# A list scheduler in place of a hand-written order, in the attention stage of an attention and routed-experts kernel

## The chip, the cores and the metric

The kernel runs on one core of one Trainium2 chip. The time is the device time of one execution in microseconds (us). The kernel before takes 1050.81 us (median of 4 runs, 1050.44 to 1051.66).

Engines: PE is TensorE's matmuls, PEld its weight loads, DVE is VectorE, ACT is ScalarE, POOL is GpSimd, SP is the engine that issues most loads. In this kernel TensorE writes its results to a memory called PSUM, in banks, and other engines copy them from there to SBUF. A name such as L247 is a line of the kernel whose profile is shown; the two kernels number their lines differently.

## The reference, cut to what matters

```python
# attention: batch 8, heads 8, 512 local and 32 global tokens, head size 64
out_g = softmax(scale * q_g @ [k_g, k_l].T) @ [v_g, v_l]          # global rows see everything
s_ll  = where(abs(i - j) <= 32, scale * q_l @ k_l.T, -1e9)         # local rows: a band of 65
out_l = softmax([scale * q_l @ k_g.T, s_ll]) @ [v_g, v_l]          #   and the 32 global keys
x = concat(out_g, out_l).reshape(4352, 512)                        # tokens x model
# routing: exp(x @ w_gate), 8 iterations of row and column normalising, P is 4352 x 8
# experts: out = sum_e P[:, e] * (relu(x @ w1[e]) @ w2[e]),  w1 512x1024, w2 1024x512
```

## The kernel before

Attention is worked off in 32 head pairs (two heads side by side); four pairs make a block, which is one batch entry. For each pair TensorE transposes q and k into one PSUM tile `pt`; ACT copies the q half and DVE the k half to SBUF; TensorE makes scores; ACT takes exponentials; DVE multiplies the band mask in; TensorE multiplies by v (`attend`); DVE normalises; TensorE transposes back to `xT`, the input of the experts.

Expert 0 needs no routing weights before its end, so its 560 big matmuls serve as filler for TensorE while attention waits for ACT and DVE. After attention come the rest of the filler, with the balancing (the 8 normalisations) hidden under it, and then experts 1 to 7, "the expert stage".

```python
def transposes(p):
    pt = ps_t.tile([P, 2, Sl], FP16, tag="t", name="pt")          # one buffer, one PSUM bank
    for so in range(4):
        nc.tensor.transpose(pt[:, 0, P * so : P * (so + 1)], nat[b, "q"][...], identity)
    for so in range(4):
        nc.tensor.transpose(pt[:, 1, P * so : P * (so + 1)], nat[b, "k"][...], identity)
    t = qkT[p] = wk.tile([P, 2, Sl], FP16, tag="qkT", bufs=3, name="qkT")
    for j, copy in enumerate((nc.scalar.copy, nc.vector.tensor_copy)):   # q by ACT, k by DVE
        copy(out=t[:, j, :]..., in_=pt[:, j, :]...)
# ... cut ...
def attend(p):                                                     # 28 small matmuls
    for i in (0, 1):
        for m in range(NM):        # 8 of 128x128 against 65 columns
            nc.tensor.matmul(po[:, i, VC * m : VC * (m + 1)], um(i, m, P * m - lo[m], P), vts[b % 2][:, j + m, :], ...)
    for m in range(NM - 1):        # 12 of 32 columns, the rims of the band
        ...
    for m in range(NM):            # 8 for the global keys
        ...
# ... cut ...
        READY = HP + 2
        DRAIN = (HP, 2 * HP)       # before blocks 1 and 2 the pipeline of pairs is emptied
        for s in range(NP + 3):
            have = b - 1 if s < 3 * HP else (s - READY) // HP      # which blocks' filler may run
            FA = 3.45 if s < 3 * HP else 2.3
            def fill_in():
                filler(FA / 4, have)                               # filler units by a credit of us
            # ... scores, fill_in, gate, transposes, fill_in, back, scores, masks, fill_in, attend ...
```

The softmax here doesn't subtract the row's maximum and nothing guards it: scores larger than these inputs give would overflow.

## Time and profile before

| stretch of the kernel before | us | what it is |
|---|---|---|
| 0 to 38.5 | 38.5 | first four pairs, no filler yet |
| 38.5 to 70.1 | 31.6 | blocks 1 and 2 start, two drains |
| 70.1 to 212.8 | 142.7 | the steady part of attention, with filler |
| 212.8 to 263.6 | 50.8 | rest of the filler, balancing hidden |
| 263.6 to 1048.8 | 785.2 | expert stage |

First the profile page of the kernel before, parts 1 and 2: busy time with its share of the span and the number of instructions, then the span in 40 equal slices, a digit being the busy share in tenths (PEclk: the granted TensorE clock in tenths).

```profile
PE 1015.0 (97%) x10063; PEld 831.2 (79%) x10063; DVE 652.3 (62%) x1366; ACT 458.5 (44%) x840; POOL 45.8 (4%) x80
...
PE   5888999999999999999999999999999999999997
...
PEclk9989999999999999999999999999999999999999
```

Next the busy time by stretch, kernel before. After the stretch and its length, each engine has its busy us with the number of instructions; PEclk is the granted clock, 1.00 being full; then come DMA share and GB/s.

```profile
core 0: us, PE busy (x) PEld busy (x) DVE busy (x) ACT busy (x) POOL busy (x), PEclk, DMA share, GB/s
0.00:38.50 38.50, 22.56 (x306) 14.17 (x306) 20.13 (x40) 16.95 (x35) 7.11 (x24) 1.00 1.06 244
38.50:70.10 31.60, 26.61 (x350) 14.75 (x349) 17.28 (x33) 17.92 (x40) 0.41 (x1) 0.84 0.67 208
70.10:212.80 142.70, 136.95 (x2022) 79.07 (x2021) 103.06 (x199) 93.07 (x208) 20.42 (x31) 1.00 0.58 155
212.80:263.60 50.80, 49.47 (x257) 24.79 (x254) 29.56 (x62) 23.97 (x46) 6.76 (x10) 1.00 0.85 180
263.60:1048.80 785.20, 779.45 (x7140) 698.38 (x7138) 482.32 (x1033) 306.62 (x511) 11.15 (x15) 1.00 0.27 74
```

The expert stage is three quarters of the time and is not touched. The clock column hides a cold phase: clock records begin at 42.8 us, and before that matmuls start at about double the distance (107 ns against 56 from one transpose of q or k to the next).

Over the whole steady part TensorE's pieces make 111.1 of the 142.7 us of the chain, DVE's 18.4 and ACT's 9.6.

The last view of the kernel before is the timeline of PE around one attend (start us, us, engine line operation). Note the starts of the lines L287 and L290.

```profile
95.01 0.42 PE L281 MATMUL po<-vt,u 128*128 128x65 f16 x8
95.36 0.20 PE L287 MATMUL po<-vt,u 128*32 128x65 f16 x1
95.36 0.20 PE L290 MATMUL po<-vt,u 128*32 128x65 f16 x1
95.40 0.20 PE L287 MATMUL po<-vt,u 128*32 128x65 f16 x1
95.40 0.20 PE L290 MATMUL po<-vt,u 128*32 128x65 f16 x1
...
95.65 0.29 PE L296 MATMUL po<-vga,ugk 32*128 32x65 f16 x8
95.88 0.31 PE L312 MATMUL gbank<-vt,u 128*32 128x65 f16 x16
```

The small matmuls start in pairs at nearly the same time and then nothing starts for about 0.03 us. The 28 matmuls from 95.01 to 95.88 us take 0.87 us, 31 ns each on average; but over the trace the median distance to the next start is 33 ns for L281, 4 ns for L287, 33 ns for L290 and 15 ns for L296, which sums to 0.61 us. Most of the rest lies where one kind of matmul follows another: by the trace 0.12 us pass from the last start of L281 (95.24) to the first of L287 (95.36), and as much again before L296 and before L312. A median over a line doesn't see these three pauses.

### The profile page before, as it was taken

How to read it: one execution, taken by the hardware profiler on the slowest of the kernel's cores; microseconds unless marked ns; L12 is line 12 of the kernel's file. 1: busy time of each engine (PE TensorE's matmuls, PEld its weight loads, DVE VectorE, ACT ScalarE, POOL GpSimd, SP SyncE). 2: the span in 40 equal slices, each digit the busy share in tenths (PEclk: the TensorE clock that was granted, in tenths of full speed). 3: DMA queues.
4: the chain of work that ended last, by engine and by line, in shares of the span. 5: the costliest groups of instructions: out<-in, count | busy, mean ns of one | idle time of the engine just before them, and what ended most of it. 6: DMA issues, size and time to landing. Idle time of an engine off the chain costs nothing.

```text
span 1048.8 us, 23363 instructions
## 1 busy us (share of the span) xinstructions
PE 1015.0 (97%) x10063; PEld 831.2 (79%) x10063; DVE 652.3 (62%) x1366; ACT 458.5 (44%) x840; POOL 45.8 (4%) x80
## 2 busy tenths in 40 slices
PE   5888999999999999999999999999999999999997
PEld 3445555544888888888888888888888888888886
DVE  5557788564455575555555555567766666666665
ACT  4456776644544444444444444433333333333332
POOL 2002020020100000000000000020000000000000
PEclk9989999999999999999999999999999999999999
DMA  9949792195821122122211121294321321321321
GB/s 260 243 127 219 232 249 73 42 195 145 159 61 62 61 61 62 61 61 61 61 62 62 62 61 61 62 179 93 92 76 56 96 72 56 95 72 56 95 73 41
DMA packets 111175, 105.33 MB, mean 100 GB/s; under 512 B 16720, under 2 KB 86368, under 8 KB 111072
## 3 DMA queue, kind: packets, MB, share of 16 engines
q1 hardware_dynamic: 85168, 77.75, 24.4%
q0 software_dynamic: 22016, 21.51, 11.7%
q10 hardware_dynamic: 3888, 4.59, 1.3%
q8 instruction: 78, 1.28, 0.5%
q14 instruction: 25, 0.20, 0.1%
HBM read 93.73 MB, written 26.88 MB: 115 GB/s over the span
## 4 chain that ended last, share of the span: by engine, by line
PE 91%; DVE 5%; ACT 2%; issue 1%; DMA 0%; DVEq 0%; SPq 0%; ACTq 0%
PE ph L601 40%; PE acc L626 34%; PE ph L109 5%; PE py L121 5%; PE sc L247 1%; DVE u L259 1%; DVE xn L303 1%; PE pt L232 1%; PE sc L251 1%; ACT u L255 1%; PE gbank L329 1%; PE pt L230 1%; PE po L281 1%; PE po L287 1%; PE po L296 0%
## 5 line engine op out<-in xcount | busy, mean ns | idle before, releaser
L603 ACT ACTIVATE h<-ph 128x512 f16<-128x512 f32 x476 | 284.1, 597 | 464.5 <-PE ph L601 432.5
L601 PE MATMUL ph<-xp,w1e 128*128 128x256 f16 x3808 | 435.0, 273 | 0.0
L601 PEld LDWEIGHTS <-w1e 128*128 128x128 f16 x3808 | 372.6, 98 | 43.3
L611 DVE TENSOR_TENSOR s<-h 128x512 f16<-128x512 f16 x595 | 210.1, 420 | 269.3 <-ACT h L603 269.3
L626 PE MATMUL acc<-wb,s 128*128 128x256 f16 x2380 | 279.3, 273 | 0.0
L626 PEld LDWEIGHTS <-s 128*128 128x128 f16 x2380 | 232.9, 98 | 26.9
L589 DVE TENSOR_TENSOR xp<-xT,pb 128x1024 f16<-128x1024 f16 x119 | 145.0, 1219 | 35.7 <-DMA pb<-ptd 35.7
L651 DVE TENSOR_TENSOR o<-o,acc 128x256 f32<-128x256 f32 (+1 forms) x306 | 134.5, 504 | 5.1 <-PE acc L626 1.5
L626 PE MATMUL acc<-wb,h 128*128 128x256 f16 x952 | 123.4, 273 | 0.0
L626 PEld LDWEIGHTS <-h 128*128 128x128 f16 x952 | 93.2, 98 | 10.8
L109 PE MATMUL ph<-xT,w 128*128 128x512 f16 (+1 forms) x288 | 73.1, 380 | 2.3 <-DVE hT L92 1.4
L121 PE MATMUL py<-w,hT 128*128 128x512 f16 x272 | 69.7, 381 | 0.9 <-ACT ys L96 0.9
L255 ACT ACTIVATE u<-sc 128x480 f16<-128x480 f32 (+1 forms) x128 | 59.5, 520 | 16.8 <-PE sc L251 16.1
L109 PEld LDWEIGHTS <-w 128*128 128x128 f16 x288 | 26.2, 101 | 27.5 <-issue 7.1
L121 PEld LDWEIGHTS <-hT 128*128 128x128 f16 x272 | 24.8, 99 | 26.0 <-issue 4.1
L90 ACT ACTIVATE hT<-ph 128x512 f16<-128x512 f32 (+1 forms) x49 | 27.6, 563 | 37.2 <-PE ph L109 33.9
L236 DVE COPY qkT<-pt 128x512 f16<-128x512 f16 x32 | 22.1, 691 | 31.1 <-ACT qkT L236 31.0
L259 DVE TENSOR_TENSOR u<-u,mask 128x704 f16<-128x704 f16 x64 | 30.9, 524 | 15.3 <-ACT u L255 15.3
L247 PE MATMUL sc<-qkT 64*128 64x160 f16 (+1 forms) x256 | 24.9, 255 | 2.8 <-ACT ugk L268 1.8
L92 DVE TENSOR_SCALAR hT<-ph 128x512 f16<-128x512 f32 x23 | 15.8, 686 | 15.9 <-PE ph L109 15.9
L330 ACT COPY xT<-gbank 128x512 f16<-128x512 f16 x32 | 18.9, 589 | 13.4 <-PE gbank L329 13.3
L155 POOL DMA_DIRECT2D w1e<-in_moe_w_dram x7 | 5.3, 764 | 432.6 <-PE ph L601 415.2
(93 smaller groups left out, 475.3 us busy)
## 6 DMA issues: line engine op xcount, KB each, us to landing
pb<-ptd SPq DMA_DIRECT2D x119, 128.0 KB, 4.0
o<-y0d SPq DMA_DIRECT2D x34, 256.0 KB, 4.1
ya<-o SPq DMA_DIRECT2D x34, 256.0 KB, 2.5
o<-ya SPq DMA_DIRECT2D x34, 256.0 KB, 3.8
out_dram<-o SPq DMA_DIRECT2D x34, 256.0 KB, 2.2
qs<-in_q_l_dram SPq DMA_DIRECT2D x7, 1024.0 KB, 9.2
ks<-in_k_l_dram SPq DMA_DIRECT2D x7, 1024.0 KB, 8.0
w1e<-in_moe_w_dram POOLq DMA_DIRECT2D x7, 1024.0 KB, 10.1
```

The lines of the kernel that those rows point to most:

```text
L90: nc.scalar.activation(out=o, in_=i, func=AF.Relu)
L109: nc.tensor.matmul(ph[:, 0:TG], w1_0[:, dk, P * fm : P * (fm + 1)], xT[:, dk, P * g0 : P * g0 + TG], start=(dk == 0), stop=(dk == DP - 1))
L121: nc.tensor.matmul(py, hTs[g][:, fk, P * c : P * (c + 1)], w2_0[:, fk, :], start=(fk == 0), stop=(fk == FT - 1))
L247: nc.tensor.matmul(pss[i][:, off[m] : off[m] + wid[m]], qkT[p][rr, 1, P * m : P * (m + 1)], qkT[p][rr, 0, lo[m] : hi[m]], start=True, stop ...
L255: nc.scalar.activation(out=u_[p][i][:, mp, :], in_=pss[i][:, 0:w], func=AF.Exp, scale=scale)
L259: nc.vector.tensor_tensor(out=u_[p][i][:, :, 0:HALF], in0=u_[p][i][:, :, 0:HALF], in1=mask, op=ALU.mult)
L589: nc.vector.tensor_tensor(out=t, in0=xT[:, :, 256 * g : 256 * (g + 1)], in1=pb.unsqueeze(1).broadcast_to([P, DP, 256]), op=ALU.mult)
L601: nc.tensor.matmul(ph[:, ff, :], w1e[:, dk, P * fm : P * (fm + 1)], xps[k][:, dk, :], start=(dk == 0), stop=(dk == DP - 1))
L603: nc.scalar.activation(out=hT[:, 2 * fp : 2 * fp + 2, :], in_=ph, func=AF.Relu)
L611: nc.vector.tensor_tensor(out=t[:, n], in0=x, in1=y, op=op)
L626: nc.tensor.matmul(acc[m // 2][:, m % 2, :], l[:, j, :], r[:, j, :], start=first, stop=(e == es[-1] and j == FK - 1), skip_group_check=True)
L651: nc.vector.tensor_tensor(out=v, in0=v, in1=i1, op=op)
```

## The change

The intent is to have the order of all instructions up to the expert stage planned instead of written by hand. Every group of instructions becomes an `Op` with an engine, a duration taken from a trace, its dependencies and the buffers it takes; a list scheduler picks the operation that can start first, and ties go to the smaller key. The drains go. Filler comes in units of two matmuls instead of four, and where ACT or DVE can do a copy, the plan takes the one that ends first. The loads of weights for experts 1 and 2 move later. Arithmetic and shapes stay, apart from finer casts.

```diff
-        READY = HP + 2
-        DRAIN = (HP, 2 * HP)
-        for s in range(NP + 3):
-            ...                                    # the hand-written order
+    def ready(o):                                  # earliest start by dependencies and buffers
+        t = 0.0
+        for x in o.deps:
+            if x.end is None:
+                return None
+            t = max(t, x.end - (x.lat if "PE" in o.eng and "PE" in x.eng else 0.0))
+        if o.alloc:
+            tag, n = o.alloc
+            ...                                    # the n-th last holder of the tag must be done
+        return t
+    def run_schedule():
+        while pending:
+            ...                                    # o = the one with the smallest (start, key)
+            free[eng] = end
+            o.end = end + o.lat
+            o.fn(*((eng,) if len(o.eng) > 1 else ()))
+    def either(act, dve):
+        return {"ACT": act, "DVE": dve}
+    def add_pair(p):
+        T[p] = op("PE", 0.45, lambda: transposes(p), k, [...], alloc=("pt", 1), lat=PEL)
+        EQ[p] = op("ACT", 0.49, lambda eng="ACT": evac_qk(eng, p, 0), k, uses=[T[p]], alloc=("qkT", 3))
+        EK[p] = op("DVE", 0.61, lambda eng="DVE": evac_qk(eng, p, 1), k, uses=[T[p]], alloc=("qkT_k", 3))
+        ...                                        # scores, exponentials, masks
+    def add_attend(p):
+        A[p] = op("PE", 0.87, lambda: attend(p), k + 0.2, [...], alloc=("po", 1), lat=PEL)
+        BK[p] = op("PE", 0.32, lambda: back(p), k + 0.3, uses=[N[p]], alloc=("xo", 1), lat=PEL)
+        EB[p] = op(either(0.49, 0.61), 0, lambda eng: copy_on(eng, xT[...], xo), k + 0.3, uses=[BK[p]])
+        ...
+    w0 = op("DMA", 6.0, load_w0, 3.6, [ops_load[1, "q", 0], ops_load[1, "k", 0]], lat=DMAL)
+    ...                                            # filler units get keys from 1000 on: last choice
```

The plan takes an attend to be 0.87 us of TensorE, and it takes `EQ` and `EK`, the copies of the q and k halves out of `pt`, to be independent of each other.

## The prediction

> **What bounds the kernel now.** The expert stage, from layer 1's first matmul (263.6 us in the chain of waits) to the end, is 785 us of back-to-back matmuls: 7,140 at a start-to-start pitch of 109 ns are 778 us. The change leaves it alone. Only the first 263.6 us can move: attention, expert 0 as filler for TensorE, and balancing.
>
> There "PE busy 97%" misleads. The Trainium skill, "Trainium Kernel Development and Optimization", section "Performance Expectations", calls matmul busy time a bad metric because matmuls are pipelined. The trace agrees: a warm 128x128 transpose is recorded as 235 ns but starts every 56 ns. Summing median start-to-start pitches gives 195 us of TensorE work in the 263.6 us (expert 0: 118 us; attention 75; balancing 2). About 69 us is waiting or cold clock:
> - 0 to 38.7 us: four head pairs and no filler; loads at 245 GB/s.
> - 38.7 to 70.1 us: two drains; clock records show half speed from 59.9 to 70.1 us, and matmuls take 389 ns before 42.8 us.
> - 70.1 to 212.9 us: 119 us of work in 142.8 us, 83%; filler waits on ACT exponentials, DVE masks and copies in a fixed order.
> - 212.9 to 263.6 us: 232 filler matmuls at 216 ns = 50.1 us. TensorE-bound; balancing (3.5 us an iteration) hides under it.
>
> **The change.** Arithmetic and shapes stay. A list scheduler, fed with durations like the trace's, fixes each engine's order. It drops both drains, halves the filler units, gives filler evacuations and some xT copies to whichever of ACT and DVE is free first, splits the q/k/v casts (DVE 746 to 765 instructions; about 0.23 us more per q or k block), and moves the weights of experts 1 and 2 later. All y stores go to POOL's queue.
>
> **Critical path.** The built order puts 224 filler matmuls after the last gate (232 before), so the tail stays: I take 50 us. The gain must come earlier.
> - Start: no filler runs until w1 of expert 0 lands (32.9 us before), and block 2 cannot start until its k lands (45 us). I expect the state now reached at 70 us at about 48 us: 20 to 22 us gained.
> - Steady part: 92% instead of 83%, 119/0.92 = 129 us: 13 us gained. Not 100%: over attention DVE needs about 122 us, ACT 118, plus 36 us of filler evacuations and 7 of combining, some 141 us each; all three engines are nearly balanced, so cross-engine waits show.
>
> Sum: 33 to 36 us, attention ending near 178 us and the expert stage starting near 229 us.
>
> **Predicted: 1016 us**, range 1003 to 1034. Faster by over 2%: 0.82; within 2%: 0.17; slower: 0.01.
>
> **What would show it.** First layer 1 matmul at 216 to 246 us, and 785 us from there to the end. Clock full from about 40 us on, no half-speed stretch at 60 us. First filler at 33 to 38 us. DVE and ACT near 80% busy from 50 to 175 us, against 72% and 65% now. Balancing still hidden.
>
> **What would make it wrong.** The planner thinks loads take 3.3 us per MB and expert 0's weights 6 us; the trace has 5 to 9 and 10 to 17, so queues fixed in a wrong order may stand behind a cast that waits for its load (q of block 2 on DVE). Combining expert 3 now stands between balancing iterations 5 and 6; if its quarters land later than about 18 us after the last gate, DVE and then TensorE stall. If the steady part stays at 83%, I lose 13 us (1029). If the planner's order fits better than I allow, 97%, the time is about 1008 us.

## More of the kernel before

In the steady part PE is recorded busy for 136.95 of 142.70 us. That number alone can't say how full TensorE is, since pipelined matmuls overlap in the record.

The chain of waits in the kernel before, from the steady part (start us, length us, what), says it more directly:

```profile
72.05 0.86 PE py L121 x4
72.91 0.26 PE sc L247 x4
73.17 0.16 PE sc L251 x2
73.33 0.86 PE ph L109 x4
74.20 0.91 PE py L121 x4
75.11 0.26 PE sc L247 x4
```

Each of these pieces starts where the last one ends, and all of them are TensorE's.

## The result, and the profile after

The changed kernel takes 1034.73 us (median of 8 runs, 1033.83 to 1035.52), and the kernel before 1051.03 us in the same rounds. The ratio is 0.9845, with a 95% interval of 0.9835 to 0.9854. Ratios here are the mean time of one kernel's fast runs over that of the other's fast runs of the same rounds, so not quite the ratio of the quoted medians. The gain is 16.3 us, 1.6%: just outside the predicted range (1003 to 1034), and less than the 2% that was given a chance of 0.82.

The profile page of the changed kernel, parts 1 and 2:

```profile
PE 1009.7 (98%) x10063; PEld 829.4 (80%) x10063; DVE 646.7 (63%) x1405; ACT 463.5 (45%) x850; POOL 53.8 (5%) x96
...
PE   5899999999999999999999999999999999999997
...
PEclk9899999999999999999999999999999999999999
```

The busy time by stretch, changed kernel, cut at the same events as before:

```profile
core 0: us, PE busy (x) PEld busy (x) DVE busy (x) ACT busy (x) POOL busy (x), PEclk, DMA share, GB/s
0.00:38.20 38.20, 25.11 (x363) 16.70 (x364) 23.09 (x51) 20.56 (x44) 6.96 (x24) 0.97 1.04 253
38.20:60.00 21.80, 20.26 (x300) 11.56 (x297) 13.24 (x34) 14.51 (x31) 0.41 (x1) 0.89 0.68 205
60.00:199.30 139.30, 137.56 (x2024) 78.74 (x2023) 99.04 (x226) 99.13 (x221) 18.87 (x30) 1.00 0.64 172
199.30:247.40 48.10, 47.13 (x249) 23.85 (x246) 29.07 (x62) 22.71 (x45) 15.86 (x25) 1.00 0.87 190
247.40:1032.80 785.40, 779.61 (x7141) 698.53 (x7139) 482.26 (x1033) 306.60 (x511) 11.71 (x16) 1.00 0.27 74
```

The expert stage starts at 247.4 us instead of 263.6 and lasts as long as before. So all of the gain lies ahead of it, as predicted. To see where, TensorE's work has to be sized. The following estimate takes, for each kind of group (8 transposes, 6 score matmuls, 28 matmuls of an attend, one filler matmul and so on), the time from its first start to the start of the next group, at full clock and as the lower quartile over the trace: 0.447 us for 8 transposes, 0.325 for a group of scores, 0.870 for an attend, 0.216 for a filler matmul (0.109 for each of the 32 narrow ones, all of them in the last stretch). Time without work, and time lost to half clock, both count as idle.

| stretch | before: us | work | idle | after: us | work | idle |
|---|---|---|---|---|---|---|
| to the first filler | 38.6 | 12.2 | 26.3 | 38.2 | 15.2 | 23.0 |
| to the same state (32.2 us of work done) | 31.5 | 20.0 | 11.5 | 21.8 | 17.0 | 4.8 |
| steady part, to the last gate | 142.7 | 131.1 | 11.6 | 139.4 | 133.1 | 6.3 |
| rest of the filler | 50.9 | 48.3 | 2.6 | 48.0 | 46.1 | 1.9 |
| sum, to the expert stage | 263.6 | 211.6 | 52.0 | 247.4 | 211.4 | 36.0 |

By this estimate 16.0 us of idle time went: 10.0 in the first two stretches, 5.3 in the steady part, 0.7 at the end. The prediction had 195 us of work and 69 us of idle time.

A second reading concerns the copies of q and k. These are groups of the two pages (line engine operation, count | busy, mean ns | idle before it, and its releaser); the first line is of the kernel before, the second of the changed one, in a fence of its own.

```profile
L236 DVE COPY qkT<-pt 128x512 f16<-128x512 f16 x32 | 22.1, 691 | 31.1 <-ACT qkT L236 31.0
```

```profile
L197 DVE COPY qkT<-pt 128x512 f16<-128x512 f16 x32 | 22.1, 690 | 18.3 <-PE pgk L259 11.3
```

In the kernel before, DVE's copy of the k half waits for ACT's copy of the q half. Both read the same PSUM tile. In the changed kernel the order is mixed: by the trace the k half goes first in 22 of 32 pairs, and then ACT waits for DVE. The two never run together: over 32 pairs the second copy starts at least 0.61 us after the first in both kernels. The chain of waits of the changed kernel shows what that does in the start (start us, length us, what):

```profile
7.44 0.50 ACT qkT L197
7.96 0.70 DVE qkT L197
...
14.61 0.59 ACT qkT L197
15.23 0.70 DVE qkT L197
15.98 1.03 PE pt L224 x8
17.08 0.59 ACT qkT L197
17.70 0.69 DVE qkT L197
...
59.12 0.59 ACT qkT L197
59.74 0.70 DVE qkT L197
```

Copy after copy, the pair stands on the chain that ended last. The plan takes them to run side by side. The Trainium skill, "PSUM — Partial Sum Buffer", section "PSUM bank collisions raise a hardware error", says that two engines must not use one bank in the same quadrant (32 partitions) at once, reads included, and advises to guard PSUM by bank. The compiled program behaves as if it did so, and the trace agrees: 0.61 us at least between the starts. (That it is the shared PSUM tile and not the shared SBUF tile `qkT` was not tried on the chip.)

### The profile page after: what moved, and what is told of

It is laid out like the page before. It is cut to its first block, busy times and chain, and to the rows that moved or that the text cites. A ratio compares the mean times of both kernels' runs of the same rounds, so it can differ in the third digit from the quotient of the medians.

```text
span 1032.8 us, 23454 instructions
## 1 busy us (share of the span) xinstructions
PE 1009.7 (98%) x10063; PEld 829.4 (80%) x10063; DVE 646.7 (63%) x1405; ACT 463.5 (45%) x850; POOL 53.8 (5%) x96
## 4 chain that ended last, share of the span: by engine, by line
PE 95%; DVE 2%; ACT 1%; issue 0%; DMA 0%; ACTq 0%; DVEq 0%
PE ph L721 40%; PE acc L746 35%; PE py L413 6%; PE ph L398 6%; PE pt L224 1%; PE sc L241 1%; PE sc L245 1%; PE po L283 1%; PE po L277 1%; PE gbank L330 1%; PE po L292 1%; DVE qkT L197 1%; PE pgk L259 1%; DMA gs<-in_k_g_dram 0%; ACT qkT L197 0%
## 5 line engine op out<-in xcount | busy, mean ns | idle before, releaser
L709 DVE TENSOR_TENSOR xp<-xT,pb 128x1024 f16<-128x1024 f16 x119 | 145.0, 1219 | 31.8 <-DMA pb<-ptd 31.8
L405 ACT ACTIVATE hT<-ph 128x512 f16<-128x512 f32 (+1 forms) x61 | 34.9, 572 | 12.0 <-PE ph L398 12.0
L253 DVE TENSOR_TENSOR u<-u,mask 128x704 f16<-128x704 f16 x64 | 31.2, 519 | 4.5 <-ACT u L250 3.9
L197 ACT COPY ys<-py 128x512 f32<-128x512 f32 x31 | 18.2, 587 | 21.3 <-PE py L413 18.6
L424 POOL DMA_DIRECT2D y0d<-ys x34 | 19.2, 564 | 162.7 <-ACT ys L197 122.7
```

The source lines that it names most:

```text
L197: (nc.scalar.copy if eng == "ACT" else nc.vector.tensor_copy)(out=out, in_=in_)
L405: nc.scalar.activation(out=o, in_=i, func=AF.Relu)
L709: nc.vector.tensor_tensor(out=t, in0=xT[:, :, 256 * g : 256 * (g + 1)], in1=pb.unsqueeze(1).broadcast_to([P, DP, 256]), op=ALU.mult)
```

## The experiments

Eighteen kernels ran. "Against the changed kernel" is worked out from ratios: (0.9845 minus the ratio) times 1051 us. Most intervals are about ±0.0015, that is ±1.6 us, so differences below 2 us settle nothing. The four columns from the trace are the first matmul of the attend of pairs 3, 4 and 8 (with the filler matmuls that were issued before it) and of the expert stage. They are of the one profiled run, so they need not follow the medians to the microsecond.

| run | us, median | ratio | against the changed kernel | pair 3 | pair 4 | pair 8 (filler) | expert stage |
|---|---|---|---|---|---|---|---|
| before | 1051.03 | 1 | | 33.7 | 50.5 | 79.3 (68) | 263.4 |
| changed | 1034.73 | 0.9845 | | 31.6 | 39.9 | 69.6 (62) | 247.4 |
| before_t2 | 1064.10 | 1.0131 | | 36.9 | 53.9 | 84.5 (68) | 276.6 |
| before_att2 | 1075.66 | 1.0234 | | 36.3 | 54.4 | 86.3 (68) | 289.3 |
| before_nodrain | 1046.28 | 0.9959 | | 34.6 | 39.2 | 67.6 (32) | 259.3 |
| after_t2 | 1047.55 | 0.9968 | 12.9 slower | 35.9 | 43.1 | 73.9 (62) | 260.6 |
| after_m2 | 1050.62 | 0.9996 | 15.9 slower | 34.6 | 42.7 | 75.7 (62) | 263.3 |
| after_m2plan | 1040.95 | 0.9904 | 6.2 slower | 29.2 | 39.6 | 69.0 (54) | 252.1 |
| after_w0small | 1034.61 | 0.9847 | 0.2 slower | 31.8 | 40.0 | 69.8 (62) | 247.6 |
| after_w0plan | 1032.94 | 0.9830 | 1.6 faster | 33.1 | 40.8 | 63.8 (38) | 245.5 |
| after_g1 | 1032.01 | 0.9824 | 2.2 faster | 33.1 | 41.0 | 69.6 (52) | 248.1 |
| after_warm | 1030.79 | 0.9808 | 3.9 faster | 31.2 | 37.9 | 66.0 (56) | 244.4 |
| after_sc4 | 1034.74 | 0.9845 | 0 | 27.6 | 39.7 | 71.6 (70) | 248.7 |
| after_best | 1031.32 | 0.9803 | 4.4 faster | 25.9 | 41.2 | 64.3 (46) | 244.2 |
| after_know | 1029.54 | 0.9801 | 4.6 faster | 29.4 | 39.3 | 66.7 (54) | 244.9 |
| after_ek | 1029.64 | 0.9802 | 4.5 faster | 29.0 | 35.3 | 64.8 (62) | 241.2 |
| after_gb | 1038.29 | 0.9885 | 4.2 slower | 34.4 | 41.1 | 72.1 (54) | 250.7 |
| after_knowwarm | 1030.08 | 0.9804 | 4.3 faster | 31.9 | 37.8 | 64.1 (54) | 242.3 |
| after_ekwarm | 1031.44 | 0.9815 | 3.2 faster | 30.3 | 37.6 | 65.4 (54) | 244.7 |
| after_eksc4 | 1031.31 | 0.9807 | 4.0 faster | 27.2 | 38.0 | 68.6 (70) | 244.3 |

Two of them, after_w0small and after_w0plan, give a wrong result on purpose (relative error 0.53, since expert 0's weights are only partly loaded). All others are correct.

### Is TensorE full in the steady part?

The transposes that open each pair are issued twice, in the kernel before and in the changed one with its order kept. That is 14.3 us more of TensorE work (32 times 8 transposes of 56 ns) and nothing for the other engines.

```diff
-            for so in range(4):
+            for so in (0, 1, 2, 3, 0, 1, 2, 3):
```

> The kernel before, with the 8 transposes that open each head pair issued twice (256 extra 128x128 matmuls, same result; a warm group of 8 takes 0.447 us in the trace, so 14.3 us of TensorE work over 32 pairs). Theory P (the prediction's: the stretch from 70 to 213 us holds only 119 us of TensorE work, 24 us are free): the free time takes most of it, +0 to +5 us. Theory N (group times from start to next start give 131 us of work there, TensorE is 92% full): +8 to +14 us.

Measured: 13.4 us more (1064.10 against 1050.70 us).

> The changed kernel with the same 256 extra transposes and every queue's order unchanged. Theory N (the part from 60 us on is 95.5% full of TensorE work): +10 to +15 us against after (1034.7), so about 1045 to 1050. Theory P (92% was a mere guess and cross-engine waits set the pace): +0 to +6 us.

Measured: 12.9 us more than the changed kernel. From the attend of pair 8 to that of pair 31, where 10.3 us were added, the kernel before goes from 126.1 to 133.9 us and the changed one from 124.8 to 133.8. Nine tenths of what is added on TensorE comes out as time over all of the kernel, in both kernels. In that steady stretch alone it is 7.8 of 10.3 us (three quarters) in the kernel before and 9.0 in the changed one; in the kernel before the start gives more than was added there (5.2 us later at pair 8). The total is in the band of theory N and outside that of theory P. But three quarters in the stretch itself leave room for argument about 83% or 92%, so a second load was tried.

What was wrong with 83%? The two sizings of TensorE's work differ most in the small matmuls. A single group decides: all 28 matmuls of an attend are issued twice into the same accumulators. The sums of the exponentials are doubled with the outputs, so the normalised result stays right.

```diff
+            for rep in (0, 1):
-                                     start=(m == 0), stop=False, skip_group_check=True)
+                                     start=(m == 0 and rep == 0), stop=False, skip_group_check=True)
...
-                                     vga[rq, 2 * b + hh, :], start=False, stop=True, ...)
+                                     vga[rq, 2 * b + hh, :], start=False, stop=(rep == 1), ...)
```

> The kernel before, with the 28 matmuls of every attend issued twice into the same accumulators. The sums of the exponentials double with the outputs, so the normalised result stays correct. By the median pitches of the prediction an attend is 0.59 us of TensorE work (18.9 us for 32), by whole groups 0.87 us (27.8 us). In the stretch from the attend of pair 8 to that of pair 31, 126.0 us before, the doubled transposes showed that about 0.8 of added work appears as time. If the median sizing is right: 136 to 140 us there, and +14 to +19 us of total time. If the sizing by groups is right: 142 to 146 us there, and +22 to +30 us of total time.

Measured: 1075.66 us, 24.8 us more, and 144.0 us from pair 8 to pair 31. Both are in the band of the sizing by groups (27.8 us of work for 32 attends) and outside that of the medians (18.9 us). In that stretch, all at full clock, 18.0 us came on top where the medians say that 13.6 us were added and the groups 20.0. In its trace a doubled attend takes 1.75 us, twice 0.87. A median sizing can't explain it: more time came than it says was added. The prediction's work sum is shown to be too small, and the attends alone make 8.9 us of the missing 17 (212 by groups less 195).

### Or are DVE and the order the limit?

The mask multiplication is issued twice in the changed kernel, with the order kept: 31 us more on DVE.

```diff
     def masks(p, i):
         nc.vector.tensor_tensor(out=u_[p][i][:, :, 0:HALF], in0=u_[p][i][:, :, 0:HALF], in1=mask, op=ALU.mult)
+        nc.vector.tensor_tensor(out=u_[p][i][:, :, 0:HALF], in0=u_[p][i][:, :, 0:HALF], in1=mask, op=ALU.mult)
```

> The changed kernel with each mask multiply done twice (64 extra DVE instructions of 0.48 us pitch, 31 us of DVE work; the mask is 0 or 1, so the result stays). Theory P (three engines nearly balanced, DVE and ACT limit the steady part together with TensorE): +10 to +25 us. Theory N (TensorE limits, DVE has room: 71% busy from 60 to 199 us): +0 to +7 us.

Measured: 1050.62 us, 15.9 us more. That looks like a rival for TensorE: half of what DVE was given comes out as time, the side of the theory called P there. But the order had been planned for short masks. The second run tells the planner.

```diff
-            M[p, i] = op("DVE", 0.445, lambda i=i: masks(p, i), k, [X[p, 1, i]], uses=[X[p, 0, i]])
+            M[p, i] = op("DVE", 0.925, lambda i=i: masks(p, i), k, [X[p, 1, i]], uses=[X[p, 0, i]])
```

> The doubled masks of after_m2 again (1050.6 us), with the planner told that a mask takes 0.925 us, so that it orders the queues for it. If after_m2's 16 us came from an order planned for short masks, most of it goes: 1036 to 1042. If DVE time itself limits the steady part, 1046 to 1052.

Measured: 1040.95 us, 6.2 us more. Ten of the 16 us went with a new order, so they were the cost of a stale order and not of DVE's time. The other 6.2 remain with an order made for them, so DVE is not the limit but not free either. Two engines each seem to be "the limit" when loaded at a fixed order: an added duration pushes both itself and everything that was planned behind it.

### What held the start back?

The drains alone, taken out of the kernel before, with the rule for which filler may run:

```diff
-        DRAIN = (HP, 2 * HP)
+        DRAIN = ()
-            have = b - 1 if s < 3 * HP else (s - READY) // HP
+            have = (s - READY) // HP
```

> The kernel before without its two drains at blocks 1 and 2 (filler of block 0 then starts two pairs later, when its rows of x are ready). If the drains cost the start what the prediction said (half of the gain of the start came from dropping them), 4 to 10 us faster than before; if the start is set by the loads and by when expert 0's weights land, within 3 us of before.

Measured: 1046.28 us, 4.4 us faster than before. Pair 8 comes 11.7 us earlier, but with 36 fewer filler matmuls done (7.8 us at 0.216), and that work has to be done later. Without a new plan the drains are worth 4 of the 16 us. The table's column with the fillers is needed for this: an early pair is no gain if filler was put off.

Loads were the first suspect for the changed kernel. In after_w0small only a quarter of expert 0's weights is loaded, the order being kept.

```diff
-        nc.gpsimd.dma_start(out=w1_0, in_=moe_w1[0].rearrange("(dko dki) f -> dki dko f", dki=P))
+        nc.gpsimd.dma_start(out=w1_0[:, 0:1], in_=moe_w1[0].rearrange("(dko dki) f -> dki dko f", dki=P)[:, 0:1])
         # the same for w2_0; the matmuls read the loaded part over and over
```

> Wrong result on purpose: of expert 0's weights only a quarter is loaded (1 MB of 4 MB read) and used for every contraction slice, so the matmuls are as many and as long and every order stays. Theory L (the start is bound by bytes: 13.4 MB at about 250 GB/s have to come in before block 2 can run): the other 3 MB are worth 12 us of loading, block 2 starts 6 to 12 us earlier where the queues' order lets it, time 4 to 10 us below after. Theory C (the start is bound by the pair chain at half clock and by the order): within 2 us of after.

Measured: no change (1034.61 us). The loads landed 5 to 11 us earlier (w1 of expert 0 at 27.8 instead of 32.9 us, its w2 at 30.0 instead of 41.4, k of block 2 at 35.8 instead of 43.9), and no attend moved by over 0.2 us. At this order the start doesn't wait for loads. In after_w0plan the planner knows of the lighter loads (1.5 us instead of 6 for each of the two).

> Wrong result on purpose: only a quarter of expert 0's weights is loaded, as in the run before that kept the order, and now the planner is told so (1.5 us instead of 6 for each of the two loads) and plans again. Theory L2 (the volume of the loads holds the start back, but through the order that is planned around it, which is why lighter loads at a fixed order gave nothing): block 2's first attend moves from 69.6 us to 60 to 65 us, and the time is 1026 to 1031. Rival: the attend of pair 8 stays within 2 us of 69.6 us and the time within 2 us of 1034.7.

Measured: pair 8 moves to 63.8 us as the load theory said, but with 24 fewer filler matmuls (5.2 us), and the time, 1032.94 us, falls on the rival's side. Loads that move a milestone and not the time are a rearrangement. The run after_g1 loads the global columns of part 1 right after block 0, ahead of block 1.

```diff
-            gload[part] = op("DMA", 0.4, lambda: load_g(part, nc.sync), key - 3, ...)
+            gload[part] = op("DMA", 0.4, lambda: load_g(part, nc.sync), key - 3 if part > 1 else 3.4, ...)
```

> The changed kernel with one load moved: the global q, k and v of batch blocks 2 and 3 (0.4 MB) go out right after block 0's loads, as in the kernel before, not behind block 2's loads. In the changed kernel block 2's scores wait for them (they land at 47 to 50 us, are cast at 58.3 us, first scores of block 2 at 61.2 us). If this placing is what keeps block 2 from starting at 48 us, its scores start 5 to 10 us earlier and the time falls 3 to 8 us; if the loads or casts of block 2 itself hold it, within 2 us of after.

Measured: 1032.01 us, 2.2 us faster by the ratios, with a wide interval (0.9803 to 0.9846), so hardly to be told from nothing. The first scores of block 2 came at 60.7 instead of 61.2 us, not 5 to 10 us earlier: this placing was not what held block 2.

The clock was the second suspect. In the changed kernel the records give full clock from 29.3 to 36.1 us, half from 36.1 to 42.9, and full from there on. The Trainium skill, "TensorE: Matmul & The Clock Gate", section "Part 1: The HAM clock gate", says that the clock is either half or full, and that a window of about 3.4 us of work or idleness decides. The trace agrees: only 0.5 and 1.0 occur, and the half-speed stretches in the starts of these runs last 3.41 us or a multiple (6.83, 10.24, 13.65, 17.07). In after_warm, 180 dummy matmuls stand in idle gaps of TensorE's plan before the first filler.

```diff
+    def warm():
+        t = ps_mm.tile([P, 512], FP32, tag="mm", name="warm")
+        for _ in range(3):
+            nc.tensor.matmul(t[:, 0:192], identity, maskP, start=True, stop=True)
+    last = None
+    for n in range(60):
+        last = op("PE", 0.24, warm, 2000.0 + n, [last], alloc=("mm", 2))
```

> The changed kernel with 180 useless 128x192 matmuls put by the planner where it sees TensorE idle before the first filler (result unchanged), to bring the clock to full speed early. In after the records show full clock only from 29.3 to 36.1 us and from 42.9 us on. Theory C (half clock costs the start several us): full clock from 5 to 10 us on, time 3 to 8 us below after. Theory L (loads bound the start): clock full early, time within 2 us of after, or a little above.

Measured: 1030.79 us, 3.9 us faster. The clock is full from 6.0 to 53.8 us, and pair 8 comes at 66.0 us with 6 fewer filler matmuls. Theory C's band holds it; but the dummies also make the planner choose another order, and this run doesn't separate the two.

The score banks were the third suspect: scores of a pair wait for the exponentials of the set before, through a single pair of PSUM banks. In after_sc4 the second set of the first six pairs takes the two banks of the filler, idle by then.

```diff
+        pool, tag = (ps_mm, "mm") if mp == 1 and p < EARLY else (ps_s, "s")
-        ps = pss[p, mp] = [ps_s.tile([P, UW], FP32, tag="s", name=f"sc{i}") for i in (0, 1)]
+        ps = pss[p, mp] = [pool.tile([P, UW], FP32, tag=tag, name=f"sc{i}") for i in (0, 1)]
```

> The changed kernel, but in the first six head pairs the second set of scores goes into the two PSUM banks of the filler matmuls, which are idle then, so that the scores need not wait for the exponentials of the set before; the planner is told and plans again. Correct results. Theory S (the start is paced by the round trip from scores to exponential and back through one pair of score banks): the attend of pair 3 starts near 28 us instead of 31.6, the expert stage 4 to 8 us earlier than 247.4, time 1027 to 1031. Theory C (half clock and unhidden waits of evacuations pace it, not the banks): within 2 us of the changed kernel, 1033 to 1037.

Measured: pair 3 at 27.6 us, as the theory said, and nothing else: pair 4 at 39.7, the time 1034.74 us. The first filler came later (41.5 instead of 38.2 us), and so did the full clock (from 45.1 us on). This theory fell as far as the time goes; that the late clock ate a gain is not excluded by this run alone.

Then three of these edits were put together (score banks, global columns, 120 dummies).

> Three edits that the runs point to, together: the second score banks in the first six pairs, the global columns of part 1 loaded right after block 0, and 120 dummy matmuls in TensorE's planned idle gaps before the first filler. Correct results. If the gains of the parts add (3.9 us by the dummies and 2.7 by the global columns were measured, the score banks 0 to 6): 1022 to 1029, faster by over 2% than the kernel before. If they remove the same wait: 1029 to 1032.

Measured: 1031.32 us. The gains don't add; it is no better than the dummies alone.

### Waits that the planner doesn't know

The planner's own times for the changed kernel can be set against the chip's: pair 0 is planned at 14.2 us and comes at 16.8, pair 7 at 48.1 and 54.8, pair 8 at 62.3 and 69.6, pair 31 at 186.3 and 194.5. The chip falls 7 us behind by pair 7, and then keeps pace (0.9 us more over the last 23 pairs). So it is in the start that the plan isn't what the chip does. In after_know the planner is told two things: the k half is copied after the q half, and the four small results in one PSUM bank wait for one another.

```diff
-        EK[p] = op("DVE", 0.61, lambda eng="DVE": evac_qk(eng, p, 1), k, uses=[T[p]], alloc=("qkT_k", 3))
+        EK[p] = op("DVE", 0.61, lambda eng="DVE": evac_qk(eng, p, 1), k, [EQ[p]], uses=[T[p]], alloc=("qkT_k", 3))
 # in four places:
-        alloc=("xo", 1)   alloc=("pog", 1)   alloc=("ptg", 1)   alloc=("pl", 1)
+        alloc=("gb", 1)   alloc=("gb", 1)    alloc=("gb", 1)    alloc=("gb", 1)
```

> The changed kernel with a planner that knows two waits that it did not know: the k half of a pair is evacuated after the q half, since the trace shows DVE waiting for ACT there, and the four small results that share one PSUM bank wait for one another. Correct results. Theory W (these unknown waits make the 7 us by which the chip is behind the plan at pair 7): 3 to 7 us faster, 1028 to 1032. Rival (the delay is the half clock and the landing times, which no order of these repairs): within 2 us of 1034.7.

Measured: 1029.54 us, 4.6 us faster, where the planner's own estimate of the end did not move (241.7 us in both). Its time for the attend of pair 31 did: 182.4 instead of 186.3 us, so part of the gain was in the plan. Which of the two was it?

> The changed kernel, the planner told of one of the two waits only: the k half of a pair is evacuated after the q half. Correct results. If this is the wait that mattered: 1029 to 1031, as with both. If the shared bank of the small results was the one: 1033 to 1036. If each does a part: 1031 to 1033.

Measured with the first edit alone (the one line of `EK`): 1029.64 us. It is this line that brings the gain.

> The changed kernel, the planner told of the other wait only: the four small results that share one PSUM bank wait for one another. Correct results. If this is the wait that mattered: 1029 to 1031. If it was the evacuation of q and k: 1033 to 1036. If each does a part: 1031 to 1033.

Measured with the second alone: 1038.29 us, 4.2 us slower than the changed kernel. None of the expected bands held it. A truer rule made a worse order here, by the plan's own times too: pair 31 is planned at 190.6 us, 4.3 later than in the changed kernel.

In after_ek pair 8 starts at 64.8 us with the same 62 filler matmuls as in the changed kernel, 4.8 us earlier. From pair 8 to pair 31 it takes 118.9 us instead of 124.8, with 20 fewer filler matmuls (4.3 us). So the gain is mostly in the start, and about 1.6 us of it in the steady part. By the trace the q half now goes first in all 32 pairs, and the copies have left the chain of waits of the start (9.2 us of its first 60 us in the changed kernel). The plan is also nearer to the chip: 2.0 us apart at pair 7 and 2.9 at pair 31, against 6.7 and 8.2. Two doubts remain. First, the wait itself didn't shrink: up to 66 us DVE waits 7.7 us for ACT's copy, where in the changed kernel the two waited 6.9 us for each other; what changed is the order around it. Second, pair 31 is planned 5.5 us earlier, and orders made from small changes of the plan scatter from 4.2 us slower to 4.6 us faster; a control, a plan changed in something that has no meaning, was not run. So the line is shown to bring 4.5 us, and that it does so by the wait is argued. The clock is not the reason: it is full from 30.0 us on in after_ek, but only from 42.4 us in after_know, which is as fast. The chain of after_ek:

```profile
9.91 29.91 DMA qs<-in_q_l_dram x2
39.84 0.43 DVE qn L197
40.27 0.45 DVE u L253
40.76 0.30 PE po L277 x4
```

What ends last there is now a load, the q of block 2, that lands at 39.8 us: its cast on DVE (`qn`) waits for it, and the mask multiplication (`u`) stands behind the cast. A chain through a load says nothing of what happened on the engines before 39.8 us.

Do the wait and the half clock add?

> Both waits told to the planner, and the 180 dummy matmuls in planned idle gaps before the first filler, which keep the clock full. Correct results. If the two losses are separate, their gains add (5.2 and 3.9 us): 1024 to 1028, faster by over 2% than the kernel before. If they are the same wait: 1029 to 1031.

Measured: 1030.08 us. No.

> The k half after the q half in the plan, and the 180 dummy matmuls in planned idle gaps before the first filler. Correct results. If half clock and evacuation wait are separate losses: 1024 to 1028. If they are one loss: within 2 us of 1029.6, and the clock full while the time stays.

Measured: 1031.44 us, with full clock from 6.4 to 57.6 us. No. The dummies bring nothing on top of this order.

> The k half after the q half in the plan, and the second score banks in the first six pairs. Correct results. If the score banks pace the start once the evacuations fit: 1024 to 1028, the first attend of block 2 before 63 us. If not: 1028 to 1032.

Measured: 1031.31 us, the first attend of block 2 at 68.6 us. The score banks bring nothing either, though here too the full clock came late (from 42.4 us on).

Seven orders (after_warm, after_best, after_know, after_ek and the last three) lie between 1029.5 and 1031.4 us, and their intervals overlap. After_ek, one line away from the changed kernel, is among the fastest, at a ratio of 0.9802 (0.9787 to 0.9816) to the kernel before. Their first filler comes between 34.8 and 42.4 us, as in the changed kernel (38.2). In after_ek 19.9 of the 29.9 us of idle time left ahead of the expert stage (241.2 us less 211.3 of work, by the sizing above) lie before the first filler. That this start, or the load at its end, is the floor near 1030 us is a reading; no run tests it.

## Why the prediction was wrong, point by point

**Right.** The expert stage stayed (785.2 and 785.4 us). The gain lay ahead of it. The tail stayed TensorE-bound: 50.8 and 48.0 us, against 50 predicted, with 232 and 224 filler matmuls after the last gate. (The fit is in part luck: "232 filler matmuls at 216 ns = 50.1 us" takes the 32 narrow ones for wide; with 109 ns for these it is 46.7.) Balancing stayed hidden, and combining expert 3 between its iterations caused no stall of over 0.3 us. The half-speed stretch at 60 us went. The first filler came at 38.2 us, at the edge of the predicted 33 to 38.

**Wrong at the root: the size of TensorE's work.** "Summing median start-to-start pitches gives 195 us of TensorE work in the 263.6 us (expert 0: 118 us; attention 75; balancing 2). About 69 us is waiting or cold clock." By whole groups it is 212 us, attention being some 92, and 52 us idle. A median of the distances misses two things: the pauses where one kind of matmul follows another (three of 0.12 us in an attend), and, where four matmuls start together, the distance from four to four. So the 32 attends are 27.8 us instead of 19, the scores of the global keys (L265) 5.2 instead of 0.2, the attends of the global rows (L312, L317) 6.1 instead of 1.3, the transposes back 10.1 instead of 7.2; scores err the other way, 20.8 instead of 25. before_att2 shows it for the attend: 18.0 us more from pair 8 to pair 31, where the median sizing adds 13.6. Two steps inherit the error.

- "70.1 to 212.9 us: 119 us of work in 142.8 us, 83%", and from it "92% instead of 83%, 119/0.92 = 129 us: 13 us gained". It was 131 us of work, 92% full to begin with. It became 133 us in 139.4, 95.5%: 5 us less idle time. Only 11.6 us were to be had. The doubled transposes, of which nine tenths came out as time over each kernel, agree.
- "I expect the state now reached at 70 us at about 48 us: 20 to 22 us gained." It was reached at 60.0 us, 10 us gained. 17.0 us of work lay between the first filler at 38.2 us and this state, so with that first filler it could not come before 55.2 us; even from 33 us, the earliest that was predicted, it would have been 50 and not 48. What was left of the possible in this stretch was 4.8 us. Two edits gained in the start, one aimed at the half clock (36.1 to 42.9 us), one at the copies out of one PSUM tile that the plan thought parallel. Each gains about 4 us, and both together no more. Each also gives a new order, so how clock, copies and order share the loss stays open.

**Wrong in detail.** "Clock full from about 40 us on" came at 42.9, after a half-speed stretch from 36.1. "DVE and ACT near 80% busy" came out as 71% each between 60 and 199 us: 99.04 and 99.13 of 139.3 us. The expert stage started at 247.4 us instead of 216 to 246. The risk named, load times in the plan that are too short, did not come true in the changed kernel (after_w0small); in after_ek the chain does run over the cast that the prediction named, q of block 2 on DVE. A wait that the plan didn't know was not named.

**The sum.** Predicted 33 to 36 us: 20 to 22 in the start, 13 in the steady part. Measured by idle time 16.0: 10.0, 5.3, and 0.7 in the tail. The mechanism, fewer idle gaps ahead of the expert stage, was right; both terms were sized by idle time that was not there.

The page that the prediction cites, "Trainium Kernel Development and Optimization", was right to distrust busy time. The replacement was the fault. The Trainium skill, "TensorE: Matmul & The Clock Gate", section "Wait — 56ns, not 53.3ns?", says that start-to-start of matmuls "never drops below ≈25 ns however small N is". Beside it medians of 4 and 15 ns ask for a second look. But the trace doesn't agree that this is a floor for every matmul: the twelve of L287 and L290, which write to two positions in the array, start 15 ns apart on average (95.36 to 95.53 us), and the 20 small matmuls of a global attend (L312, L317) take 0.385 us, 19 ns each. A low median is no error in itself; only the time of the whole group says what the group costs.

## What to carry to other kernels

Before a gain is predicted from idle time, size the engine's work by whole groups, from the first start to the start of the next group, and hold it against the chain of waits: where the chain is one engine's back-to-back work, there is little to gain. If it is in doubt, double a group and measure. When a planner orders the instructions, compare its own times with the chip's at a few milestones; where they part there may be a wait that it doesn't know, and here one line that told it gained 4.5 us more. Run a plan with a meaningless change beside it, to know how much orders scatter; that was not done here. And load an engine in an experiment with an order planned for the load: ten of the 16 us that doubled masks cost were the stale order's.

## What the Trainium skill lacked or had wrong

- "TensorE: Matmul & The Clock Gate", section "Wait — 56ns, not 53.3ns?", states its floor of 25 ns without the exception of matmuls at different positions in the array, which the page treats in another part. Here 20 of them take 0.385 us, 19 ns each.
- No page gives a number for going from one kind of small matmul to another. Here it is 0.12 us from the last start of one to the first of the next, three times in an attend of 0.87 us.
- "Perfetto Trace Analysis", section "Identifying the Most-Contended Engine", offers weight-load busy time, among other things, to judge how far TensorE is from its limit. In the steady part before it was 79.07 of 142.70 us, 55%, where TensorE was about 92% full by whole groups (an estimate), and where 18.0 us came of 20.0 us of added attends.
- "PSUM — Partial Sum Buffer" has the rule that keeps two engines off one bank but no number for its price. Here two copies out of one bank, 0.59 us on ACT and 0.69 us on DVE, start at least 0.61 us apart, and telling the planner brought 4.5 us. (The two also write one SBUF tile; which of the two tiles keeps them apart was not tried.)
- No page says that waits added by such rules must be told to one's own planner, or that a planned order is brittle: 31 us of DVE work cost 15.9 us at the old order and 6.2 us at one planned for it.
